# Batch 7's first product as seven half products over two column blocks, and batch 4's attention three slots earlier

## The chip, the cores and the metric

The kernel runs on one core of one Trainium2 chip. The metric is the device time of one execution in microseconds (us), the median over runs. Engines are named as in the profile: PE (matmul; PEld its weight loads), DVE (VectorE), ACT (ScalarE), POOL (GpSimd), SP (SyncE, which issues most DMAs).

## The reference

Eight batches of cosine-weighted linear attention, and then a mixer. Sequence 576, 8 heads of 64, model width 512, inner width 2048, rank 32.

```python
# attention, per batch and head (c, s: cos and sin of the position)
q_p = concat([relu(q) * c, relu(q) * s]);  k_p = concat([relu(k) * c, relu(k) * s])
kv = k_p.T @ v;  z = sum_s(k_p)
x = (q_p @ kv) / (q_p @ z + 1e-6)
# mixer, on x of shape [8, 576, 512]
h = x.transpose(0, 2, 1) @ U @ V          # U [576, 32], V [32, 576]
u = x + h.transpose(0, 2, 1)
out = u + relu(u @ w_ch1) @ w_ch2         # w_ch1 [512, 2048], w_ch2 [2048, 512]
```

The two products with w_ch1 ("first product") and w_ch2 ("second product") are nearly all of the matmul work.

## The kernel before

A batch's 576 rows are held as four chunks of 128 rows and a tail of 64; the tails of two batches make one block of 128 (a "pair", pr). All matmul operands are bf16, sums are fp32 in PSUM.

For each batch the attention makes q_p and k_p (`q_prep`, `k_prep`: DVE, ACT) from staged inputs `qst`, `kst`, `vst`; `v_prep` casts v to `v_ext` on POOL; SP issues DMA transposes of q_p (`qtr_dma`); `kv_unit` and `x_unit` are matmuls with their evacuation; `A_unit`, `u_mm` and `u_add` add the low-rank term and give u (`u_bf`, on DVE); `utr_dma` transposes u into `uT` (two DMAs, halves of the 512 columns); `u_tail` and `utr_dma(b, 4, 5)` do the same for the tails. `loads(b + 1)` issues the next batch's inputs on SP.

The first product of a batch (`g1_main`, L571) runs over 16 blocks j of 128 inner columns: four matmuls of 512 columns into one PSUM bank, then one ReLU on ACT (L580) into `hid`. `g1_tail` (L605) does a pair's tail: four groups of 16 matmuls of 128 columns, each into a bank of the "g" ring, each with one ReLU (L612).

The second product of batches 2 to 7 and of the last tails is already a scheme of Strassen and Winograd: `half_part` (L772) is one of seven half products of eight matmuls with 256 columns; `hid_sum` (L717) makes the sums of `hid` on DVE that it needs (S1, S2, and two in place); a join on DVE (L730) adds each half product to u.

The order is written by hand. `slots` is a list of thunks for PE's main work, one after the other; `todo` (filled by `put`) hangs other work behind a slot; `PLAN[b]` gives for each batch the slot w of its first `kv_unit` and the offsets of the rest, where a batch's q work begins at w - 20 and its u transposes follow w + 17. Batches 3 to 7 alternate: two blocks of `g1_main(b)`, then in turn one `half_part` of batch b - 1 and one block of `g1_main(b)`; after odd batches come four tail slots. Then the second product of batch 7 runs alone, and last that of the tails. Slot 88 is the first of batch 3's, 126 of batch 4's, 156, 190 and 220 of batches 5, 6 and 7.

Every engine works its queue in order. PSUM has eight banks: "g0", "g1" (ring of the first product), "g2" and "T" (attention), "o0", "o1" (second product), and the two of "X". A PSUM tile is one unit for waiting: who writes it next waits for all that read it.

Of the kernel before, what the change touches and what calls it, by code (L numbers as in the profile page):

```python
# [10 lines left out]
FP32 = mybir.dt.float32  # L11
BF16 = mybir.dt.bfloat16
AF = mybir.ActivationFunctionType
ALU = mybir.AluOpType
# [3 lines left out]
def kernel(  # L18
# [11 lines left out]
    nc = tc.nc  # L30

    B = 8
    H = 8
    S = 576
    D = 64
    E = D + 1
    P = 128
# [3 lines left out]
    NJ = DH // P  # L41
    NPAIR = B // 2
# [31 lines left out]
    ps = Banks()  # L74
# [1 line left out]
    ctx.enter_context(tc.manual_schedule())  # L76


    qst = const.tile([P, H, 5, D], FP32)
    kst = const.tile([P, H, 5, D], FP32)  # L80
    vst = const.tile([P, H, 5, D], FP32)

    def nines(src, b):
        return src[b].rearrange("h (m k) d -> m h (k d)", k=9)
# [25 lines left out]
    w1_bf = const.tile([P, 4, DH], BF16)  # L110
# [15 lines left out]
    def cast(eng, o, i):  # L126
        if eng is nc.scalar:
            nc.scalar.activation(out=o, in_=i, func=AF.Copy, bias=0.0, scale=1.0)
        else:
            eng.tensor_copy(out=o, in_=i)  # L130


    V_, A_, G_ = nc.vector, nc.scalar, nc.gpsimd
# [30 lines left out]
    def load_uv():  # L164
# [16 lines left out]
        out=iota[:, 0:4], pattern=[[2, 4]], base=0, channel_multiplier=9,  # L181
        allow_small_or_imprecise_dtypes=True,
    )
    for lo in (0, TS):
        nc.gpsimd.iota(
            out=iota[lo : lo + TS, 4:5], pattern=[[1, 1]], base=8, channel_multiplier=18,
# [3 lines left out]
        out=iota[:, 5:6], pattern=[[1, 1]], base=8, channel_multiplier=9,  # L190
# [85 lines left out]
    k_p, q_p, q_pT, kv_sb, x_bf = {}, {}, {}, {}, {}  # L276
    u_bf, u_tl, uT, uT_tl = {}, {}, {}, {}
# [279 lines left out]
    hid, hid_tl = {}, {}  # L557
# [35 lines left out]
                stop=False,  # L593
            )

    def g1_tail(pr, jq):
        if pr not in hid_tl:
            hid_tl[pr] = pool.tile(
                [P, NJ, P], BF16, tag="q_p" if pr == 3 else "hid_tl", bufs=1, name="hid_tl"
            )  # L600
        g_ps = ps.tile([P, 4, P], FP32, tag="g", bufs=3, name="gt_ps")
        for jj in range(4):
            j = jq * 4 + jj
            for d in range(4):
                nc.tensor.matmul(  # L605
                    out=g_ps[:, jj, :],
                    lhsT=w1_bf[:, d, j * P : j * P + P],
                    rhs=uT_tl[pr][:, d, :],
                    start=(d == 0),
                    stop=(d == 3),  # L610
                )
        nc.scalar.activation(  # L612
            out=hid_tl[pr][:, jq * 4 : jq * 4 + 4, :], in_=g_ps, func=AF.Relu,
            bias=0.0, scale=1.0,
        )
# [78 lines left out]
    def h_of(b, half, c):  # L694
        if b == B:
            return hid_tl[2 + c // 2][:, half * 8 : half * 8 + 8, :]
        return hid[b][:, half * 8 : half * 8 + 8, c * P : c * P + P]
# [45 lines left out]
    def half_part(b, n, k, form):  # L743


        c2 = n + 2
        i = ORDER[form][k]
        if k == 0:
            halves[b, n] = {
                "o": [  # L750
                    pool.tile([P, DM], FP32, tag="o_sb", bufs=8, name="o_sb") for _ in range(2)
                ]
            }
            if form == "alone":
# [12 lines left out]
        at = BANKS[form].get(i)  # L767
        if at is not None:
            w[to] = bank(at)
        acc = w[to][:, 0:256]  # L770
        for j in range(8):
            nc.tensor.matmul(  # L772
                out=acc, lhsT=lhs[:, j, :], rhs=rhs[:, j, :],
                start=(j == 0 and at is not None), stop=(j == 7),
                skip_group_check=at is None,
            )
        lo, hi = slice(0, 256), slice(256, 512)
        o, o2 = w["o"]
        u = [[u_of(b, c, g) for g in range(2)] for c in (n, c2)]

        def first(t, cs, c, g):
            add(V_, by_n(t[:, cs]), u[c][g], by_n(acc))

        def more(t, cs):
            add(V_, t[:, cs], t[:, cs], acc)

        if form == "alone":
            ss = w["s"]
            if i == 1:
                cast(A_, ss[:, lo], acc)  # L790
            elif i == 2:
                first(o, lo, 0, 0)
            elif i == 5:
                cast(A_, o2[:, hi], acc)
            elif i == 6:
                cast(A_, ss[:, hi], acc)
            elif i == 4:
                cast(A_, o2[:, lo], acc)
                add(G_, by_n(o2), by_n(o2), u_bf[b][:, :, c2, :])
            elif i == 3:  # L800
                first(o, hi, 0, 1)
                add(G_, o, o, ss)
            elif i == 7:
                o2v = o2.rearrange("p (g n) -> p g n", g=2)
                add(V_, o2v, o2v, acc.unsqueeze(1).to_broadcast([P, 2, 256]))
        elif i == 1:
            first(o, lo, 0, 0)
        elif i == 2:
            more(o, lo)
        elif i == 6:  # L810
            first(o, hi, 0, 1)
        elif i == 5:
            first(o2, hi, 1, 1)
        elif i == 3:
            more(o, hi)
        elif i == 4:
            first(o2, lo, 1, 0)
        else:
            if form == "last":
                more(o2, lo)  # L820
            more(o2, hi)
        if i == 2:
            hid_sum(b, n, 4)
        if k == 6:
# [37 lines left out]
    def spare(at):  # L862
# [8 lines left out]
    PLAN = {  # L871
        2: (46, -15, V_, V_, -10, (-5, -4, -4)),
        3: (64, -12, V_, A_, -7, (3, 3, 18)),
        4: (100, (-20, 1, V_, V_), (-13, 2, A_, V_), -12, (-9, -4, -4)),
        5: (127, (-24, 2, A_, A_), (-14, 2, A_, V_), -14, (-8, -4, -4)),
        6: (157, (-24, 2, A_, A_), (-14, 2, A_, V_), -14, (-8, -4, -4)),
        7: (191, (-24, 2, A_, A_), (-14, 2, A_, V_), -14, ()),
# [218 lines left out]
    for c in TL:  # L1096
        k_prep(0, c, FEATS[c])
        for h in range(H):
            nc.tensor.matmul(  # L1099
                out=z_ps[:, h : h + 1], lhsT=k_of(0, c, h), rhs=v_tl[:, 0, D:E],  # L1100
                start=(c == 0 and h == 0), stop=(c == 4 and h == H - 1),
            )
        if c < 4:
            nc.tensor.matmul(
                out=z_all[:, 1, :], lhsT=zero[:, 0:P], rhs=zero, start=True, stop=True
# [108 lines left out]
    def tail_out(pr):  # L1214
        slots.extend(lambda p=p: g2_part(pr, 4, p) for p in range(4))
# [10 lines left out]
    slots += [g1(2, j) for j in range(NJ)]  # L1226
    put(len(slots) - 1, lambda: ps.give("g", ("g0", "g1")))
    alone = len(slots)
    for b in range(3, B):
        at = len(slots)  # L1230
        sums(b - 1, 0, (at, at + 1, at + 3))
        sums(b - 1, 1, (at + 5, at + 7, at + 9) if b == 3 else (at + 13, at + 15, at + 19))
        slots += [g1(b, 0), g1(b, 1)]
        for n in range(2):
            for i7 in range(7):
                slots.append(lambda b=b, n=n, i7=i7: half_part(b - 1, n, i7, "with g"))
                if i7 > 4:
                    put(len(slots), lambda b=b, n=n, i7=i7: half_store(b - 1, n, i7 - 5))
                slots.append(g1(b, 2 + 7 * n + i7))
        if b % 2:  # L1240
            tail_slots(b // 2)
        if b == 3:
            tail_out(b // 2)
    at = len(slots)
    sums(B - 1, 0, range(at - 4, at - 1))
    sums(B - 1, 1, (at + 1, at + 3, at + 5))
    sums(B, 0, (at + 8, at + 10, at + 11))
    put(at - 1, lambda: ring.append("g2"))
    for n in range(2):
# [11 lines left out]
    at = len(slots)  # L1261
# [57 lines left out]
```

## Time and profile before

| | |
|---|---|
| median of 3 runs | 297.73 us (296.2 to 298.64) |
| profiled execution | 296.4 us, span 294.6 us |
| PE | 286.1 us busy (97% of the span) |
| DVE, ACT, POOL | 192.6, 154.7 and 51.1 us busy |
| clock that PE was granted | 1.0 throughout |
| matmuls of the first product, 128x512 | 0.379 us each, four in 0.86 us of the chain |
| matmuls of the second product, 128x256 | 0.273 us each, eight in 0.87 us of the chain |

A matmul's recorded duration holds its way through the array and overlaps with the next; what counts for PE is the step from one to the next. The chain of waits is followed back from the last instruction: at each step to what released it. "Idle before, releaser" tells how long an engine sat idle before an instruction and who ended it. A window's row gives busy time and counts of the engines in that stretch of the span.

### The profile page before, as it was taken

Reading aid. Unit: us, or ns where it says so; the run is one execution under the profiler, and the core shown is the slowest. Engines: PE = TensorE matmul, PEld = TensorE weight load, DVE = VectorE, ACT = ScalarE, POOL = GpSimd, SP = SyncE. Lnnn points to the kernel's source line nnn. Section 1 sums busy time; section 2 is a strip of 40 time slices with the busy share of each in tenths; the row PEclk is TensorE's granted clock in tenths of the full one; section 3 lists DMA queues with packets and bytes.
Section 4 is the critical chain, followed back from the end, with each engine's and each line's share of the span. In section 5 each row is a group of like instructions: output and inputs, shape, how many; then the busy total and the mean of one; then the engine's idle time right before and its main releaser. Section 6 shows DMA issues by size and latency. Waiting matters only on the chain.

```text
span 294.6 us, 6987 instructions
## 1 busy us (share of the span) xinstructions
PE 286.1 (97%) x2832; PEld 189.4 (64%) x2874; DVE 192.6 (65%) x459; ACT 154.7 (53%) x281; POOL 51.1 (17%) x89
## 2 busy tenths in 40 slices
PE   8999999999999999999989999999999999999995
PEld 6685464447645445676757666766877666668884
DVE  4978656684798887657546794678437755344563
ACT  2956842175880467577826865378743234334310
POOL 8800400012030002500500411031200100000340
PEclk9999999999999999999999999999999999999999
DMA  6999999799998999999989659952900141001013
GB/s 212 330 261 254 261 205 216 173 305 249 280 192 135 283 244 238 234 312 289 232 198 309 162 116 271 289 182 60 246 2 3 73 120 43 36 36 75 2 71 142
DMA packets 90707, 54.05 MB, mean 183 GB/s; under 512 B 58420, under 2 KB 87380, under 8 KB 90676
## 3 DMA queue, kind: packets, MB, share of 16 engines
q1 hardware_dynamic: 84116, 43.85, 62.4%
q0 software_dynamic: 6416, 9.63, 14.0%
q8 instruction: 22, 0.36, 0.5%
q10 hardware_dynamic: 144, 0.13, 0.1%
q14 instruction: 9, 0.07, 0.1%
HBM read 36.86 MB, written 9.44 MB: 157 GB/s over the span
## 4 chain that ended last, share of the span: by engine, by line
PE 94%; DVE 1%; DMA 1%; issue 1%; ACT 1%; SPq 0%; DVEq 0%
PE g_ps L571 36%; PE h_ps L772 27%; PE o_ps L643 10%; PE gt_ps L605 4%; PE w_ps L228 3%; PE kv_ps L342 3%; PE x_ps L417 3%; DMA uT<-u_bf 1%; PE a_ps L440 1%; PE t_ps L372 1%; PE va_ps L470 1%; PE t_ps L360 1%; PE g_ps L588 1%; DVE x_bf L427 0%; PE z_ps L1099 0%
## 5 line engine op out<-in xcount | busy, mean ns | idle before, releaser
L580 ACT ACTIVATE hid<-g_ps 128x512 bf16<-128x512 f32 x128 | 76.2, 597 | 100.9 <-PE g_ps L571 99.4
L571 PE MATMUL g_ps<-uT,w_bf 128*128 128x512 bf16 x474 | 121.1, 379 | 2.3 <-DMA uT<-u_bf 0.9
L571 PEld LDWEIGHTS <-w_bf 128*128 128x128 bf16 x504 | 47.5, 98 | 42.6 <-issue 1.1
L772 PEld LDWEIGHTS <-hid 128*128 128x128 bf16 x480 | 45.4, 98 | 11.8
L730 DVE TENSOR_TENSOR o_sb<-u_bf,h_ps 128x256 f32<-128x256 bf16 x44 | 18.4, 417 | 31.7 <-PE h_ps L772 31.5
L772 PE MATMUL h_ps<-w_bf,hid 128*128 128x256 bf16 x288 | 37.0, 273 | 0.1
L643 PE MATMUL o_ps<-w_bf,hid 128*128 128x512 bf16 x122 | 29.5, 379 | 0.4 <-issue 0.2
L130 POOL CAST v_ext<-vst 128x512 bf16<-128x512 f32 (+1 forms) x26 | 18.3, 729 | 57.3 <-DMA vst<-in_v_dram 46.8
L730 DVE TENSOR_TENSOR o_sb<-o_sb,h_ps 128x256 f32<-128x256 f32 (+1 forms) x36 | 15.5, 432 | 18.7 <-PE h_ps L772 18.5
L772 PE MATMUL h_ps<-w_s,S 128*128 128x256 bf16 x208 | 26.5, 273 | 0.0
L772 PE MATMUL h_ps<-w_s,hid 128*128 128x256 bf16 x192 | 24.9, 272 | 0.0
L830 POOL DMA_DIRECT2D out_dram<-o_sb x16 | 10.0, 625 | 84.4 <-DVE o_sb L730 83.0
L772 PEld LDWEIGHTS <-S 128*128 128x128 bf16 x208 | 19.9, 98 | 5.2
L478 DVE TENSOR_TENSOR u_bf<-x_bf,va_ps 128x512 bf16<-128x512 bf16 x27 | 17.8, 679 | 6.5 <-PE va_ps L470 4.2
L643 PEld LDWEIGHTS <-hid 128*128 128x128 bf16 x128 | 11.6, 98 | 12.5
L427 DVE TENSOR_TENSOR x_bf<-x_ps,rec 128x512 bf16<-128x512 f32 x22 | 15.2, 691 | 0.8
L605 PE MATMUL gt_ps<-uT_tl,w_bf 128*128 128x128 bf16 x256 | 15.6, 219 | 0.0
L605 PEld LDWEIGHTS <-w_bf 128*128 128x128 bf16 x256 | 14.7, 98 | 1.2
L301 ACT ACTIVATE k_p<-kst,cosw 128x512 bf16<-128x512 f32 x20 | 14.2, 713 | 0.4 <-DVE rec L408 0.4
L301 ACT ACTIVATE q_p<-qst,sinw 128x512 bf16<-128x512 f32 x18 | 12.6, 710 | 2.4 <-DMA qst<-in_q_dram 2.4
L303 DVE TENSOR_SCALAR k_p<-kst,sinw 128x512 bf16<-128x512 f32 x23 | 12.7, 554 | 0.0
L342 PEld LDWEIGHTS <-k_p 128*128 128x128 bf16 x240 | 10.5, 97 | 2.6
(170 smaller groups left out, 351.1 us busy)
## 6 DMA issues: line engine op xcount, KB each, us to landing
qst<-in_q_dram SPq DMA_DIRECT2D x14, 512.0 KB, 5.6
kst<-in_k_dram SPq DMA_DIRECT2D x14, 512.0 KB, 8.0
vst<-in_v_dram SPq DMA_DIRECT2D x12, 512.0 KB, 7.9
out_dram<-o_sb POOLq DMA_DIRECT2D x19, 256.0 KB, 3.4
w_bf<-in_moe_w_ch_dram POOLq DMA_DIRECT2D x8, 512.0 KB, 13.1
out_dram<-o_sb SPq DMA_DIRECT2D x16, 256.0 KB, 2.4
qst<-in_q_dram SPq DMA_DIRECT2D x2, 640.0 KB, 8.8
kst<-in_k_dram SPq DMA_DIRECT2D x2, 640.0 KB, 8.3
```

Source lines behind the costliest of these rows:

```text
L130: eng.tensor_copy(out=o, in_=i)
L301: nc.scalar.activation(out=o, in_=i, func=AF.Relu, bias=0.0, scale=w)
L303: eng.tensor_scalar(out=o, in0=i, scalar1=0.0, scalar2=w, op0=ALU.max, op1=ALU.mult)
L342: nc.tensor.matmul(out=acc[:, i, :], lhsT=k_of(b, c, h), rhs=v_tl[:, h, 0:n] if c == 4 and b < 2 else vx[:, c if c < 4 else 4 + b % 2, h, ...
L427: nc.vector.tensor_tensor(out=x_of(b, c, rows).rearrange("p (g i d) -> p g i d", g=2, d=D), in0=view[:, :, :, 0:D], in1=rec[rows].unsqueez ...
L478: nc.vector.tensor_tensor(out=u_bf[b][:, j, :, :], in0=x_bf[b][:, :, ns], in1=va[b][j].rearrange("p (c n) -> p c n", c=4), op=ALU.add,)
L571: nc.tensor.matmul(out=g_ps.rearrange("p (c t) -> p c t", c=4), lhsT=w1_bf[:, d, j * P : j * P + P], rhs=uT[b][:, d, :, :], start=(d == 0) ...
L580: nc.scalar.activation(out=hid[b][:, j, :], in_=g_ps, func=AF.Relu, bias=0.0, scale=1.0)
L605: nc.tensor.matmul(out=g_ps[:, jj, :], lhsT=w1_bf[:, d, j * P : j * P + P], rhs=uT_tl[pr][:, d, :], start=(d == 0), stop=(d == 3),)
L643: nc.tensor.matmul(out=o[:, cols], lhsT=lhs[:, j, c * P : c * P + P], rhs=w2_bf[:, j, cols], start=(j == 0), stop=(j == NJ - 1),)
L730: eng.tensor_tensor(out=o, in0=x, in1=y, op=ALU.add)
L772: nc.tensor.matmul(out=acc, lhsT=lhs[:, j, :], rhs=rhs[:, j, :], start=(j == 0 and at is not None), stop=(j == 7), skip_group_check=at is ...
```

## The change

Three things change.

1. Batch 7's first product. Blocks p and p + 8 are taken together with the two halves of the 512 rows and the two halves of the 512 inner indices d: seven half products (`g1_cross`) of two matmuls with 256 columns each, in place of eight matmuls with 512. They go into X and Y (the halves of one bank) and Z (half of another); even p use "g0" and "g1", odd p "g2" and "T". `g1_join` copies three of the partial results out (P1, U2, P5, on ACT), adds them to the others on DVE (C11, C22, C12), and makes the ReLUs (two on ACT, one clamp of 512 on DVE). Each group issues two or more half products of pair p and the rest of pair p - 1; between the groups stand batch 6's half parts, and between the last four groups the four tail blocks, which now lie two by two in the tile "X".
2. The sums that this needs: four of w_ch1 in two halves each (`w1_sum`, DVE, in slots 186 to 215) and four of uT (`uT_sum`, DVE, slots 218 to 221). They lie in the staging tiles of q, k and v, which batch 7 has read by then; the copies lie in the dead `q_pT`. For that the staging tiles come from the work pool.
3. In `PLAN`, batch 4's w goes from 100 to 97, with all that hangs on it.

```diff
-    qst = const.tile([P, H, 5, D], FP32)
-    kst = const.tile([P, H, 5, D], FP32)
-    vst = const.tile([P, H, 5, D], FP32)
+    qst, kst, vst = [
+        pool.tile([P, H, 5, D], FP32, tag=name, bufs=1, name=name)
+        for name in ("qst", "kst", "vst")
+    ]
...
+    W1 = [
+        w1_bf[:, 0:2, 0:1024], w1_bf[:, 2:4, 0:1024],
+        w1_bf[:, 0:2, 1024:2048], w1_bf[:, 2:4, 1024:2048],
+    ]
+    def w1_sum(i, half):
...
+        x, y, op = {
+            1: lambda: (W1[2], W1[3], ALU.add),
+            2: lambda: (w1_s[1], W1[0], ALU.subtract),
+            3: lambda: (W1[0], W1[2], ALU.subtract),
+            4: lambda: (W1[1], w1_s[2], ALU.subtract),
+        }[i]()
+        cs = slice(512 * half, 512 * half + 512)
+        diff(w1_s[i][:, :, cs], x[:, :, cs], y[:, :, cs], op)
...
+    CROSS = [("g0", "g1"), ("g2", "T")]
+    def g1_cross(b, p, i):
...
+            xy, z = [
+                psum.tile([P, 512], FP32, tag=tag, bufs=1, name="c_ps") for tag in CROSS[p % 2]
+            ]
+            cross[b, p] = {"X": xy[:, 0:256], "Y": xy[:, 256:512], "Z": z[:, 0:256]}
...
+        to, lhs, rhs, first = {
+            1: lambda: ("X", W1[0], uT_quarter(b, 0, 0), True),
+            2: lambda: ("Y", W1[1], uT_quarter(b, 1, 0), False),
+            3: lambda: ("Z", w1_s[4], uT_quarter(b, 1, 1), False),
+            4: lambda: ("X", W1[3], uT_s[b, 4], False),
+            5: lambda: ("Z", w1_s[1], uT_s[b, 1], True),
+            6: lambda: ("X", w1_s[2], uT_s[b, 2], False),
+            7: lambda: ("X", w1_s[3], uT_s[b, 3], False),
+        }[i]()
+        for d in range(2):
+            nc.tensor.matmul(
+                out=w[to].rearrange("p (c t) -> p c t", c=2), lhsT=lhs[:, d, cs],
+                rhs=rhs[:, d], start=(first and d == 0), stop=(d == 1),
+                skip_group_check=not first,
+            )
+    def g1_join(b, p, i):
+        w, lo, hi = cross[b, p], slice(0, 256), slice(256, 512)
+        top, low = hid[b][:, p, :], hid[b][:, p + 8, :]
...
+        if i == "C11":
+            diff(top[:, lo], w["P1"], w["Y"], ALU.add)
+        elif i == "C22":
+            diff(low[:, hi], w["P5"], w["X"], ALU.add)
+            relu(low[:, hi], low[:, hi])
+        elif i == "C12":
+            diff(top[:, hi], w["U2"], w["Z"], ALU.add)
+            relu(low[:, lo], w["X"])
+            V_.tensor_scalar(out=top, in0=top, scalar1=0.0, scalar2=None, op0=ALU.max)
+        else:
...
+            cast(A_, w[i], w["Z" if i == "P5" else "X"])
...
-        4: (100, (-20, 1, V_, V_), (-13, 2, A_, V_), -12, (-9, -4, -4)),
+        4: (97, (-20, 1, V_, V_), (-13, 2, A_, V_), -12, (-9, -4, -4)),
...
+    for i, half, sl in (
+        (1, 0, -4), (1, 1, -3), (3, 0, -3), (3, 1, -2), (2, 0, -1), (2, 1, 21), (4, 0, 22), (4, 1, 25),
+    ):
+        put(at - 30 + sl, lambda i=i, half=half: w1_sum(i, half))
+    for i in range(4):
+        put(at - 2 + i, lambda i=i: uT_sum(b7, i + 1))
...
+    def opened(p):      # products 1, 2; then P1, C11
+    def second(p):      # products 6, 5; then U2, P5
+    def third(p):       # product 7; then C22
+    def closed(p):      # products 3, 4; then C12
...
+    groups = [
+        group(p, *fs) for p in range(9) for fs in ((opened, third), (second, closed))
+    ]
...
+    def tail_cross(j):
+        if j % 2 == 0:
+            x_tail["t"] = ps.tile([P, 2, 512], FP32, tag="X", bufs=1, name="gt_ps")
...
+    for i, go in enumerate(groups):
+        slots.append(go)
+        if i < 14:
+            n, i7 = halfs[i]
+            slots.append(lambda n=n, i7=i7: half_part(b7 - 1, n, i7, "with g"))
...
+        else:
+            slots.append(lambda j=i - 14: tail_cross(j))
```

In the diff the four functions `opened` to `closed` are shortened to what they issue; `group(p, first, then)` runs `first(p)` and then `then(p - 1)`.

More of the change, by code (lines that the diff above doesn't have):

```diff
@@ L594, in g_half, with diff @@
             )
-    def g1_tail(pr, jq):
+    W1 = [
+        w1_bf[:, 0:2, 0:1024], w1_bf[:, 2:4, 0:1024],
+        w1_bf[:, 0:2, 1024:2048], w1_bf[:, 2:4, 1024:2048],
+    ]
+    w1_s, uT_s, cross = {}, {}, {}
+    def diff(o, x, y, op=ALU.subtract):
+        V_.tensor_tensor(out=o, in0=x, in1=y, op=op)
+    def w1_sum(i, half):
+        if i not in w1_s:
+            t = pool.tile(
+                [P, 2, 2, 1024], BF16, tag="qst" if i < 3 else "kst", bufs=1, name="w1_s"
+            )
+            for n in (0, 1):
+                w1_s[(i - 1) // 2 * 2 + 1 + n] = t[:, n]
+        x, y, op = {
[6 more added lines that the diff above has]
+        diff(w1_s[i][:, :, cs], x[:, :, cs], y[:, :, cs], op)
@@ new lines, in uT_quarter, with uT_sum @@
+    def uT_quarter(b, d, n):
+        return uT[b][:, 2 * d : 2 * d + 2, 2 * n : 2 * n + 2, :]
+    def uT_sum(b, i):
+        if i == 1:
+            t = pool.tile([P, 4, 2, 2, P], BF16, tag="vst", bufs=1, name="uT_s")
+            for n in range(4):
+                uT_s[b, n + 1] = t[:, n]
+        x, y = {
+            1: lambda: (uT_quarter(b, 0, 1), uT_quarter(b, 0, 0)),
+            2: lambda: (uT_quarter(b, 1, 1), uT_s[b, 1]),
+            3: lambda: (uT_quarter(b, 1, 1), uT_quarter(b, 0, 1)),
+            4: lambda: (uT_quarter(b, 1, 0), uT_s[b, 2]),
+        }[i]()
+        diff(uT_s[b, i], x, y)
@@ new lines @@
+    CROSS = [("g0", "g1"), ("g2", "T")]
+    def g1_cross(b, p, i):
+        if (b, p) not in cross:
+            if b not in hid:
+                hid[b] = pool.tile([P, NJ, 512], BF16, tag="hid", bufs=2, name="hid")
+            xy, z = [
+                psum.tile([P, 512], FP32, tag=tag, bufs=1, name="c_ps") for tag in CROSS[p % 2]
+            ]
+            cross[b, p] = {"X": xy[:, 0:256], "Y": xy[:, 256:512], "Z": z[:, 0:256]}
+        w = cross[b, p]
+        cs = slice(p * P, p * P + P)
+        to, lhs, rhs, first = {
[6 more added lines that the diff above has]
+            7: lambda: ("X", w1_s[3], uT_s[b, 3], False),
+        }[i]()
+        for d in range(2):
[3 more added lines that the diff above has]
+                skip_group_check=not first,
+            )
@@ new lines, in g1_join, with relu @@
+    def g1_join(b, p, i):
+        w, lo, hi = cross[b, p], slice(0, 256), slice(256, 512)
+        top, low = hid[b][:, p, :], hid[b][:, p + 8, :]
+        def relu(o, x):
+            nc.scalar.activation(out=o, in_=x, func=AF.Relu, bias=0.0, scale=1.0)
+        if i == "C11":
[8 more added lines that the diff above has]
+        else:
+            if (b, "kept") not in cross:
+                cross[b, "kept"] = pool.tile([P, 2, 3, 256], FP32, tag="q_pT", bufs=1, name="kept")
+            n = ("P1", "U2", "P5").index(i)
+            w[i] = cross[b, "kept"][:, p % 2, n]
+            cast(A_, w[i], w["Z" if i == "P5" else "X"])
@@ L597, in g1_tail @@
+    def g1_tail(pr, jq, g_ps=None):
         if pr not in hid_tl:
@@ L600, in g1_tail @@
             )
-        g_ps = ps.tile([P, 4, P], FP32, tag="g", bufs=3, name="gt_ps")
+        if g_ps is None:
+            g_ps = ps.tile([P, 4, P], FP32, tag="g", bufs=3, name="gt_ps")
         for jj in range(4):
@@ L1228 @@
     alone = len(slots)
-    for b in range(3, B):
+    for b in range(3, B - 1):
         at = len(slots)
@@ L1244, with group, go @@
     at = len(slots)
-    sums(B - 1, 0, range(at - 4, at - 1))
-    sums(B - 1, 1, (at + 1, at + 3, at + 5))
+    b7 = B - 1
+    for i, half, sl in (
[4 more added lines that the diff above has]
+        put(at - 2 + i, lambda i=i: uT_sum(b7, i + 1))
+    sums(b7 - 1, 0, (at, at + 1, at + 3))
+    sums(b7 - 1, 1, (at + 13, at + 15, at + 19))
+    def opened(p):
+        g1_cross(b7, p, 1)
+        g1_cross(b7, p, 2)
+        g1_join(b7, p, "P1")
+        g1_join(b7, p, "C11")
+    def second(p):
+        g1_cross(b7, p, 6)
+        g1_cross(b7, p, 5)
+        g1_join(b7, p, "U2")
+        g1_join(b7, p, "P5")
+    def third(p):
+        g1_cross(b7, p, 7)
+        g1_join(b7, p, "C22")
+    def closed(p):
+        g1_cross(b7, p, 3)
+        g1_cross(b7, p, 4)
+        g1_join(b7, p, "C12")
+    def group(p, first, then):
+        def go():
+            if p < 8:
+                first(p)
+            if p > 0:
+                then(p - 1)
+        return go
+    groups = [
+        group(p, *fs) for p in range(9) for fs in ((opened, third), (second, closed))
+    ]
+    halfs = [(n, i7) for n in range(2) for i7 in range(7)]
+    x_tail = {}
+    def tail_cross(j):
+        if j % 2 == 0:
+            x_tail["t"] = ps.tile([P, 2, 512], FP32, tag="X", bufs=1, name="gt_ps")
+        g1_tail(
+            NPAIR - 1, j, x_tail["t"][:, j % 2].rearrange("p (j t) -> p j t", j=4)
+        )
+    for i, go in enumerate(groups):
[3 more added lines that the diff above has]
+            slots.append(lambda n=n, i7=i7: half_part(b7 - 1, n, i7, "with g"))
+            if i7 > 4:
+                put(len(slots), lambda n=n, i7=i7: half_store(b7 - 1, n, i7 - 5))
+        else:
+            slots.append(lambda j=i - 14: tail_cross(j))
+    at = len(slots)
+    sums(b7, 0, (at - 1, at - 1, at))
+    sums(b7, 1, (at + 1, at + 3, at + 5))
     sums(B, 0, (at + 8, at + 10, at + 11))
```

## Prediction

> **What bounds the kernel now.** I read the page first (busy time, the chain that ended last), then what PE waited for, then tables by stage, then the two stages that the change touches in order of time.
>
> ```profile
> span 294.6 us, 6987 instructions
> PE 286.1 (97%) x2832; PEld 189.4 (64%) x2874; DVE 192.6 (65%) x459; ACT 154.7 (53%) x281; POOL 51.1 (17%) x89
> PE 94%; DVE 1%; DMA 1%; issue 1%; ACT 1%; SPq 0%; DVEq 0%
> ```
>
> PE is the bound: 94% of the chain, 97% busy. A matmul removed anywhere saves its issue time, but only if PE does not wait instead.
>
> ```profile
> PE g_ps L571 <- DMA uT<-u_bf: 0.9, 1, 0.9
> ```
>
> This is the only long PE wait after the first 2 us: 0.86 us at 149.8, where batch 4's first product waits for its second transposed half.
>
> The table by stage (us, then busy time and count of PE, PEld, DVE, ACT, POOL, clock, DMA share, GB/s): batch 7's first product beside batch 6's second, the tail blocks, and batch 7's second product alone.
>
> ```profile
> 242.10:269.20 27.10, 26.89 (x181) 17.80 (x184) 11.31 (x23) 9.55 (x16) 0.63 (x1) 1.00 0.13 50
> 269.20:272.80 3.60, 3.60 (x66) 3.59 (x64) 1.99 (x3) 2.39 (x4) 0.00 (x0) 1.00 0.20 75
> 272.80:291.20 18.40, 18.31 (x168) 16.17 (x166) 11.66 (x23) 3.67 (x9) 5.21 (x4) 1.00 0.17 65
> ```
>
> PE has no gap in the first, VectorE (DVE) and ScalarE (ACT) are idle for over half of it: that is the room the change wants to fill. The next view is ACT and DVE at its end:
>
> ```profile
> 269.24 0.60 ACT L580 ACTIVATE hid<-g_ps 128x512 bf16<-128x512 f32 x1 [1.14 <-PE g_ps L571]
> 270.13 0.60 ACT L612 ACTIVATE hid_tl<-gt_ps 128x512 bf16<-128x512 f32 x1 [0.30 <-PE gt_ps L605]
> 270.59 0.69 DVE L717 TENSOR_TENSOR S<-S,hid 128x1024 bf16<-128x1024 bf16 x1
> 271.20 0.69 DVE L717 TENSOR_TENSOR hid<-hid 128x1024 bf16<-128x1024 bf16 x1
> 273.68 0.38 ACT L128 ACTIVATE s_sb<-h_ps 128x256 f32<-128x256 f32 x1 [0.28 <-PE h_ps L772]
> ```
>
> Prices read here: ACT 0.60 for 128x512 and 0.38 for 128x256; ACT starts 0.20 after the issue of the last matmul ended (269.24 against 269.04, where the next group starts); a DVE sum of 1024 takes 0.69, but the next starts after 0.61, so 0.08 overlaps. The join of 128x256 (L730) is 0.42, so 0.34 in a queue. From ACT's end to DVE's start 0.03 is seen (243.79 to 243.82); towards PE I take 0.06.
>
> **The change part by part.**
>
> *Fewer columns.* Removed: 64 matmuls of 512 columns, 0.86 per four in the chain of waits (0.216 each), 13.8 us. Added: per pair of blocks seven half products of two matmuls with 256 columns, 112 in all, at 0.87 per eight (0.109, h_ps L772), 12.2 us. The 48 extra weight loads of 0.098 lie under 0.109 of matmul, as L772's do already. **-1.6 us**, if PE never waits.
>
> *More work per pair.* Instead of two ReLUs (1.2 us ACT) a pair gets three copies and two ReLUs on ACT (about 1.9) and three adds and one clamp on DVE. The clamp (512 bf16 in place) isn't in the trace: between 0.34 (half of a 1024 sum) and 0.47 (L303, 512 from f32); I take 0.35, nearer the bf16 row. DVE gets 8 x (3 x 0.42 + 0.35) + 4 x 0.42 = 14.6 us of recorded time on top of 11.31 in a stage of 25.5: full but for its overlaps. Every join now stands in that queue.
>
> *The pair's loop.* The order of instructions shows that product 6 waits for DVE: the sum C11, which needs the copy P1, which needs product 2. From product 2's issue: 0.20 + 0.38 + 0.03 + 0.42 + 0.06 = 1.09. PE's cover: product 7 of the pair before (0.22) and a half part (0.87) = 1.09. So about 0.02 per pair, and 0.1 in two pairs where a sum of `hid` (0.61) stands in front of C11. **+0.2**; bounds 0 (each step 0.05 shorter) and 0.27 a pair, 2.2 in all (each 0.05 longer).
>
> The Trainium skill, PSUM — Partial Sum Buffer, section "PSUM bank collisions raise a hardware error", says that two engines must not be in one bank at once and that waits go by bank, not by address. X and Y share a bank here, and the waits of the order are by bank, so the page speaks against this placing. Waits by address would drop C11 from the loop, and with it the two group starts below, some 1.4 us; no run shows it yet.
>
> *Start of the stage.* In group 0, ACT's 0.60 ReLU of batch 6's last block stands ahead of P1: product 6 comes 0.3 late. Then DVE has, from C11(0): C11, a sum of uT, S1, a join, a sum of uT, S2, a join, two sums of hid, C11(1): 0.34 + 0.34 + 0.61 + 0.34 + 0.34 + 0.61 + 0.34 + 0.61 + 0.61 + 0.42 = 4.6 us. PE meanwhile has 4 + 8 + 6 + 8 matmuls, 2.8 us, from 0.48 on. So it waits 4.6 + 0.06 - 3.3 = **1.3**, of it some 0.3 for S2 before the third half part and 1.0 at product 6 of pair 1. The uT sums (512 bf16) are unseen: 0.35 to 0.69, I take 0.42, near half the 1024 row; at 0.69, 0.5 more. Sum of both: **+1.6**, bounds 1.0 and 2.4.
>
> *Tail blocks.* Before, each took a ring bank of its own. Now two share one tile of two banks, and the order has the second, third and fourth wait for ACT, each for the ReLU of the block just before. After a block's last issue that is 0.20 + 0.60 + 0.06 = 0.86. PE's cover: two matmuls (0.22) before block 3, four (0.44) before block 4: waits of 0.64 and 0.42. Before block 2 there are eight (0.87), but ACT reaches ReLU 1 late, behind P1, C11, C22 and its clamp: 0.35. **+1.4**, bounds 1.1 and 1.7.
>
> *Sums of w_ch1.* Eight DVE sums of 1024, 0.61 each, in slots 186 to 215. The first five lie in and around batch 5's tail blocks, where DVE is busy 1.44 of 3.8 us; nothing waits. Without that cover S1 and S2 of batch 5 would be late by up to 3 us. Two stand before batch 7's last u_add: that ended at 237.84, and the tail product that needs its bank came at 238.46. 1.2 more, less 0.3 of idle in between, less 0.62: **+0.3**, bounds 0 and 0.6. uT's second transpose goes out 0.9 later on SP, still under a half part and product 1. The staging itself was dead.
>
> *Batch 4 three units sooner.* All its q and k work, three q transposes, kv, x, A, u and two u transposes move three slots (2.6 us) up, past batch 3's u_adds on DVE and, on SP, ahead of batch 5's second q transpose. The wait of 0.86 goes. But batch 4's v is not moved:
>
> ```profile
> 109.52 0.62 SPq L106 DMA_DIRECT2D vst<-in_v_dram  x1
> 110.24 0.61 SPq L93 DMA_DIRECT2D vst<-in_v_dram  x1
> 110.90 0.63 SPq L100 DMA_DIRECT2D vst<-in_v_dram  x1
> 117.11 3.94 POOL L130 CAST v_ext<-vst 128x512 bf16<-128x512 f32 x4 [2.82 <-DMA vst<-in_v_dram]
> ```
>
> POOL ends the casts at 121.05; kv came at 123.51 and will now be due at 120.9. And batch 3's u_adds now have two more pairs of q work (4 x 0.39) between them on DVE: its second u transpose leaves SP 1.6 later, batch 3's first product may wait 0 to 0.55 for it (I take 0.25), and v's loads, next on SP, land 0 to 1.6 later (DMA share there is over 1.0). Kv, and all of PE behind it, waits 0.1 to 1.7; I take 0.8. Net -0.86 + 0.25 + 0.8 = **+0.2**, bounds -0.8 and +1.4.
>
> Sum: -1.6 + 0.2 + 1.6 + 1.4 + 0.3 + 0.2 = **+2.1**. The profiled execution took 296.4 us (span 294.6 and 1.8 around it), so 298.5 on its own footing; the median of the runs shown is 297.73, 1.3 more, so **299.8**.
>
> **Rivals.**
> - *The waits are covered* (0.20): DVE and ACT run tighter than my queue sums, or PE's waits release sooner. For it: DVE idle for 16 us of the stage, and a loop that just closes. Against: the tail blocks' order, which no speed of DVE cures. Saved 1.6 + 0.86: 295.3 by the median, not slower.
> - *The pair's loop decides* (0.18): each of its steps 0.05 longer, which it is from 1.09 us on; product 6 then waits 0.27 in every pair, and the joins behind C11 follow. For: no slack at all. Against: prices without scatter in the rows. 2.0 more: 301.8, slower.
> - *Batch 4's v decides* (0.14): loads 1.6 late and casts as slow as now; kv waits 1.7, and x, A and u behind it give back what came sooner. For: DMA share over 1.0. Against: loads of 512 KB landed in 5.6 us at the median. 1.2 to 1.6 more: 301.2.
>
> **How the numbers follow.** The forecast, +0.9 to +3.0, has 0.48. One per cent, about what a measurement can tell here, is 3.0 us. Faster by that needs every wait covered and more: 0.04. Slower by that: the two slow rivals (0.32) and the upper end of the forecast (0.04): 0.36. The rest is 0.60. Range: down to a sum of lower bounds plus some scatter of the runs (296.2 to 298.64), 296.9; up past both slow rivals, 302.9.
>
> **What would show it.** Right: PE's waits after 240 name ACT hid_tl (three, together 1.4) and DVE hid (the largest, 1 us, in pair 1); the wait for uT at 149.8 gone; a new one of kv for POOL near 121; DVE near 25 us busy in the 25 to 29 us of the stage. Wrong: PE without gaps there (first rival); equal waits of 0.2 or more at product 6 in all eight pairs (second); over 1.5 at kv (third). The forecast falls if batch 7's stage, tail blocks included, takes no longer than the 30.7 us from 242.1 to 272.8.

## The result and the profile after

The changed kernel takes 298.4 us (median), the kernel before in the same comparison 296.79: a ratio of 1.0059, 95% interval 1.0034 to 1.0083, or 1.0 to 2.5 us more. Forecast were 2.1 us more, which lies inside this interval. The forecast of 299.8 us was 1.4 too high: 0.9 of that is the base (297.73 from three runs, 296.79 from twenty), 0.5 is the change. The profiled execution of the changed kernel, 300.97 us (span 299.2), was one of its slower ones, so it is read by stages and not by its total.

The page's first lines and its chain of waits:

```profile
span 299.2 us, 7180 instructions
PE 286.4 (96%) x2885; PEld 194.2 (65%) x2922; DVE 210.6 (70%) x503; ACT 157.6 (53%) x305; POOL 52.7 (18%) x89
PE 82%; DVE 7%; DMA 4%; issue 3%; ACT 1%; POOL 1%; SPq 1%; DVEq 0%; POOLq 0%; ACTq 0%
```

PE's share of the chain fell from 94% to 82%, DVE's rose from 1% to 7%. PE now waits for others, though for less than these shares suggest: it is still busy for 96% of the span. For whom, is in the list of PE's waits (us in total, times, longest):

```profile
PE g_ps L572 <- DMA uT<-u_bf: 2.2, 1, 2.2
...
PE gt_ps L706 <- ACT hid_tl L713: 0.9, 3, 0.5
PE c_ps L666 <- DVE hid L604: 0.8, 1, 0.8
PE kv_ps L343 <- POOL v_ext L131: 0.6, 1, 0.6
```

Three waits for `hid_tl` (tail blocks), one for `hid` (C11 of pair 1) and one of kv for the casts of v were named in the prediction. The first line was not: the wait for batch 4's `uT` should have gone, and it grew from 0.9 to 2.2. These times count from the modelled end of the last matmul; in steps of PE's issue a wait is 0.15 to 0.2 longer.

The table by stage, same columns as before. In the kernel before, batch 7's first product from 243.00, and its last tail blocks:

```profile
243.00:268.90 25.90, 25.69 (x173) 17.20 (x176) 10.89 (x22) 9.55 (x16) 0.63 (x1) 1.00 0.11 43
269.04:272.61 3.57, 3.57 (x66) 3.57 (x64) 1.99 (x3) 2.39 (x4) 0.00 (x0) 1.00 0.20 76
```

In the changed kernel, the groups, then from the first tail block on:

```profile
245.86:270.61 24.75, 23.75 (x212) 20.44 (x210) 19.96 (x51) 11.24 (x34) 0.63 (x1) 1.00 0.12 45
270.61:277.17 6.56, 5.61 (x80) 4.96 (x78) 3.07 (x8) 3.99 (x10) 0.00 (x0) 1.00 0.12 48
```

From the start of batch 7's first product (245.86; before 243.00, the block ahead at 242.13 and its 0.87) to the first matmul of the second product alone (277.17; before 272.61), the stage takes 31.31 us, before 29.61. That is 1.70 more; the prediction's terms for it, -1.6 + 0.2 + 1.6 + 1.4, make 1.6. DVE is busy for 23.0 us of it (19.96 + 3.07).

DVE's queue at the start of the stage, in order of time:

```profile
246.96 0.42 DVE L604 TENSOR_TENSOR hid<-kept,c_ps 128x256 bf16<-128x256 f32 x1 [0.55 <-ACT kept L129]
247.30 0.42 DVE L604 TENSOR_TENSOR uT_s<-uT 128x512 bf16<-128x512 bf16 x1
247.63 0.69 DVE L818 TENSOR_TENSOR S<-hid 128x1024 bf16<-128x1024 bf16 x1
...
248.91 0.68 DVE L818 TENSOR_TENSOR S<-S,hid 128x1024 bf16<-128x1024 bf16 x1
...
250.44 0.68 DVE L818 TENSOR_TENSOR hid<-hid 128x1024 bf16<-128x1024 bf16 x1
251.04 0.74 DVE L604 TENSOR_TENSOR hid<-kept,c_ps 128x256 bf16<-128x256 f32 x2
```

Each starts when the one before is done, without idle time, from C11 of pair 0 (246.96) to C11 of pair 1 (251.04 to 251.46): 4.5 us. PE's steps against it: product 6 of pair 0 issues at 247.44, 0.28 after the half part before it ended; the third half part waits 0.25 for S2; product 6 of pair 1 issues at 251.51, 0.99 after PE was done. Sum 1.52.

In the pairs behind, the wait for C11 stays, but is short. Pair 3:

```profile
257.24 1.04 PE L873 MATMUL h_ps<-w_s,hid 128*128 128x256 bf16 x8
258.17 0.60 PE L666 MATMUL c_ps<-uT_s,w_s 128*128 128x256 bf16 x4
```

The half part is issued by 258.11 (257.24 + 0.87), and product 6 follows 0.06 later. It is 0.06 to 0.08 in each of the pairs 2 to 6 and 0.04 in pair 7, together 0.38. The list of waits has none of these, since they end before the modelled end of the last matmul. From product 2's issue to product 6 this loop takes 1.15 (257.02 to 258.17), against a cover of 1.09 (product 7 of the pair before, 0.22, and the half part, 0.87).

The 0.28 of pair 0 is the same loop, and no matter of DVE's queue. No product 7 of an earlier pair stands in its way, so the cover is one half part, 0.87, and 1.15 - 0.87 = 0.28. The prediction laid it to ACT's ReLU of batch 6's last block. But P1 starts 0.26 after product 2's issue there (246.29 to 246.55), just as in pair 3 (257.02 to 257.28), where no ReLU stands ahead.

The tail blocks, in the chain of waits:

```profile
272.19 0.57 ACT hid_tl L713
...
272.80 1.07 PE gt_ps L706 x16
...
273.89 0.61 ACT hid_tl L713
...
274.54 1.07 PE gt_ps L706 x16
...
275.63 0.61 ACT hid_tl L713
```

Every block starts 0.04 after the ReLU of the block before. By PE's issue the three waits are 0.39, 0.63 and 0.41, together 1.43.

### The profile page after: what moved, and what is told of

Read it like the earlier page. It is cut to its first block, busy times and chain, and to the rows that moved or that the text cites. A ratio compares the mean times of both kernels' runs of the same rounds, so it can differ in the third digit from the quotient of the medians.

```text
span 299.2 us, 7180 instructions
## 1 busy us (share of the span) xinstructions
PE 286.4 (96%) x2885; PEld 194.2 (65%) x2922; DVE 210.6 (70%) x503; ACT 157.6 (53%) x305; POOL 52.7 (18%) x89
## 4 chain that ended last, share of the span: by engine, by line
PE 82%; DVE 7%; DMA 4%; issue 3%; ACT 1%; POOL 1%; SPq 1%; DVEq 0%; POOLq 0%; ACTq 0%
PE g_ps L572 27%; PE h_ps L873 25%; PE o_ps L744 8%; PE gt_ps L706 4%; PE c_ps L666 3%; PE kv_ps L343 3%; PE w_ps L229 3%; PE x_ps L418 3%; DMA vst<-in_v_dram 2%; DMA uT<-u_bf 2%; DVE q_p L304 2%; PE a_ps L441 1%; POOL v_ext L131 1%; DVE k_p L304 1%; ACT hid_tl L713 1%
## 5 line engine op out<-in xcount | busy, mean ns | idle before, releaser
L581 ACT ACTIVATE hid<-g_ps 128x512 bf16<-128x512 f32 x112 | 66.5, 597 | 88.8 <-PE g_ps L572 88.4
L572 PE MATMUL g_ps<-uT,w_bf 128*128 128x512 bf16 x415 | 105.3, 379 | 3.5 <-DMA uT<-u_bf 2.2
L572 PEld LDWEIGHTS <-w_bf 128*128 128x128 bf16 x440 | 41.9, 98 | 39.4 <-issue 2.8
L131 POOL CAST v_ext<-vst 128x512 bf16<-128x512 f32 (+1 forms) x26 | 20.0, 795 | 52.5 <-DMA vst<-in_v_dram 49.5
L706 PEld LDWEIGHTS <-w_bf 128*128 128x128 bf16 x256 | 15.0, 98 | 2.5 <-issue 1.5
L604 DVE TENSOR_TENSOR hid<-kept,c_ps 128x256 bf16<-128x256 f32 x24 | 9.4, 418 | 6.4 <-PE c_ps L666 3.8
L408 DVE TENSOR_SCALAR rec<-x_ps 128x8 f32<-128x8 f32 (+2 forms) x39 | 6.3, 162 | 10.6 <-PE x_ps L418 9.7
```

The source lines that it names most:

```text
L572: nc.tensor.matmul(out=g_ps.rearrange("p (c t) -> p c t", c=4), lhsT=w1_bf[:, d, j * P : j * P + P], rhs=uT[b][:, d, :, :], start=(d == 0) ...
L581: nc.scalar.activation(out=hid[b][:, j, :], in_=g_ps, func=AF.Relu, bias=0.0, scale=1.0)
L604: V_.tensor_tensor(out=o, in0=x, in1=y, op=op)
L706: nc.tensor.matmul(out=g_ps[:, jj, :], lhsT=w1_bf[:, d, j * P : j * P + P], rhs=uT_tl[pr][:, d, :], start=(d == 0), stop=(d == 3),)
```

## The experiments

"Stage" is the stretch of batch 7 just measured: 29.61 us before, 31.31 in the changed kernel. In `q5_later`, whose order is the changed kernel's from batch 6 on, it is 31.30, while medians move by some tenths; so small terms are read from the stage and not from the median.

**Which part costs: `b4_back` and `only_b4`.**

```diff
# b4_back, from the changed kernel
-        4: (97, (-20, 1, V_, V_), ...
+        4: (100, (-20, 1, V_, V_), ...
# only_b4, from the kernel before
-        4: (100, (-20, 1, V_, V_), ...
+        4: (97, (-20, 1, V_, V_), ...
```

> The changed kernel with batch 4's w back at 100; the half products, the sums and the tail blocks stay. Theory A, the sum of the prediction: batch 4's move is worth +0.2 us, the rest +1.9, so this is 1.9 us over the kernel before (ratio 1.006), and batch 7's stage with its tail blocks takes 31.3 us as in the changed kernel. Rival B: the profiled execution of the changed kernel is typical, where 1.9 us were lost around batch 4; then the half products are nearly even, and this is within 0.5 us of the kernel before (ratio below 1.002).

> The kernel before with one edit: batch 4's w at 97. Theory A: +0.2 us (ratio 1.0007): the wait of 0.86 for the second transposed half goes, and waits of about the same size come at batch 3's first product and at kv. Rival B: the wait doesn't go, it grows, since on SP a transpose of batch 5's q now stands between the two transposes of batch 4's u: +1.9 us (ratio 1.006), with PE's longest wait 1.5 to 2.5 us at batch 4's first product.

Measured: `b4_back` 298.58 us, ratio 1.0054 (1.0026 to 1.0083); `only_b4` 297.58 us, ratio 1.0025 (1.0005 to 1.0044). Rival B falls for the first: without batch 4's move the kernel is as slow as with it, and its stage takes 31.59 us. The 1.9 us lost around batch 4 in the changed kernel's profile are not typical. In `only_b4`, +0.7 us lies between A and B; its profile has one of theory A's two new waits, kv's. The other, at batch 3's first product, isn't there, and the wait for uT, which was to go, has only shrunk from 0.86:

```profile
PE kv_ps L342 <- POOL v_ext L130: 0.7, 1, 0.7
PE g_ps L571 <- DMA uT<-u_bf: 0.4, 1, 0.4
```

**The tail blocks: `tail_banks`.**

```diff
-        if j % 2 == 0:
-            x_tail["t"] = ps.tile([P, 2, 512], FP32, tag="X", ...)
-        g1_tail(NPAIR - 1, j, x_tail["t"][:, j % 2].rearrange(...))
+        if j in (1, 2):
+            t = psum.tile([P, 512], FP32, tag=("o0", "o1")[j - 1], ...)
+        else:
+            t = ps.tile([P, 2, 512], FP32, tag="X", ...)[:, 0]
+        g1_tail(NPAIR - 1, j, t.rearrange(...))
```

> The changed kernel with the four tail blocks in banks that don't wait for one another: the first and last in tile X, the second and third in o0 and o1, which batch 6's last half products have left. Theory A: the tail blocks' waits for the ReLU of the block before (hid_tl) are 1.4 us of PE's time; all go, and batch 7's stage falls from 31.3 to 29.9 us, the time by 1.4 (ratio 1.001 to the kernel before). Rival: ACT, which has two copies, two ReLUs and the tail's ReLU in each of these groups, is the bound there, so PE waits at the next half product for a copy instead, and less than 0.5 us is saved.

Measured: 296.62 us, ratio 0.9997 (0.9969 to 1.0025). All three waits for `hid_tl` are gone, the stage is 29.87 us, 1.44 less. ACT is not the bound there; the shared tile was.

**The transposes of batch 4's u: `q5_later`.**

```diff
-        5: (127, (-24, 2, A_, A_), (-14, 2, A_, V_), -14, ...
+        5: (127, (-24, 2, A_, A_), (-14, 2, A_, V_), -12, ...
```

> The changed kernel with batch 5's three q transposes two slots later, so that on SP none of the two long ones stands between the two transposes of batch 4's u. Theory: the second u transpose leaves SP within 1.5 us of the first (3.9 us in the changed kernel's trace, before 147.5), the wait of 2.2 us at batch 4's first product goes, and the time falls by 0.9 to 2.2 us (ratio 0.999 to 1.003). Rival: the transposes land late for another reason (queue of the DMA engines, u_adds on DVE), or batch 5's x units wait for their q instead: the time stays within 0.4 us of the changed kernel.

Measured: 297.9 us, ratio 1.0021 (1.0 to 1.0043); the wait for uT is gone, the second transpose leaves SP 2.8 us after the first (theory had 1.5), with only the short one of the tails between. But `tail_banks`, which has the changed kernel's order up to the tail blocks, has no such wait either. SP's transposes there in the changed kernel, and then in `tail_banks`:

```profile
142.27 1.23 SPq L514 DMA_TRANSPOSE uT<-u_bf  x1
143.61 3.82 SPq L387 DMA_TRANSPOSE q_pT<-q_p  x1
147.52 1.86 SPq L514 DMA_TRANSPOSE uT<-u_bf  x1
```

```profile
141.20 1.23 SPq L514 DMA_TRANSPOSE uT<-u_bf  x1
142.53 2.36 SPq L387 DMA_TRANSPOSE q_pT<-q_p  x1
144.98 1.41 SPq L514 DMA_TRANSPOSE uT<-u_bf  x1
```

The transpose of batch 5's q between them holds SP for 3.82 us in one execution and 2.36 in the other (1.83 in `start_order`, below), and the second u transpose goes out that much later. So the order theory names the right place, but what it costs varies from run to run: in the profiles with w at 97 (the two of `v_early` aside) the wait for uT was 2.2, 0.4, 0.5, 0.7 and three times under 0.2 (`q5_later` is one of these); with w at 100, 0.9, 0.3, 0.2 and 0.2. The gain of `q5_later` can't be told from this variation.

The hold on SP is only a part of it. The chain of waits has the way of the second u transpose from leaving SP to its landing, in the kernel before and in the changed one:

```profile
146.53 4.10 DMA uT<-u_bf
```

```profile
147.52 5.76 DMA uT<-u_bf
```

PE was done, and began to wait, at 149.82 (150.68 less 0.86) in the first and at 151.14 (153.32 less 2.18) in the second. So the transpose left 3.3 us ahead of that in the kernel before and 3.6 ahead in the changed one: no later for PE, but 1.7 us longer on its way. The other profiles say the same: from its leaving SP to PE's waiting matmul it is 4.15 to 4.51 us in the four with w at 100, and 5.18 to 6.31 in the five with w at 97 that show a wait there (`tail_banks`' is 0.09; the two of `v_early` aside). `y_bank` and `q5_later`, which don't wait, show only that it is under 4.9 and 5.9. With w at 97 a long transpose of batch 5's q leaves SP right behind it (149.47 in the changed kernel); with w at 100 both have left before. That the two then share the DMA engines would explain the longer way, but no run separates this.

**The start of the stage: `start_short` and `start_order`**, both from `tail_banks`.

```diff
# both: the third sum of batch 6's hid, behind C11 of pair 1
-    sums(b7 - 1, 0, (at, at + 1, at + 3))
+    sums(b7 - 1, 0, (at, at + 1, at + 4))
# start_short: uT's sums 3 and 4 on POOL (in uT_sum)
-        diff(uT_s[b, i], x, y)
+        (V_ if i < 3 else G_).tensor_tensor(out=uT_s[b, i], in0=x, in1=y, ...)
# start_order instead: uT's sums 2 to 4 in one go, in slot 219
-        put(at - 2 + i, lambda i=i: uT_sum(b7, i + 1))
+        put(at - 2 + (i > 0), lambda i=i: uT_sum(b7, i + 1))
```

> The kernel tail_banks with two edits to DVE's queue at the start of batch 7's stage: the sums 3 and 4 of uT go to POOL, and the third sum of batch 6's hid is put behind the sum C11 of pair 1. Theory, the prediction's queue of 4.6 us: it falls by 0.34 + 0.34 + 0.61 = 1.3, the wait of product 6 in pair 1 (0.8 us recorded, 1.0 in all) goes, and the time falls by 1.0 us against tail_banks, to 0.996 of the kernel before. Rival: POOL makes these sums slowly (its casts of the same size take 0.98 us) and product 7 of pair 0 waits for them, or DVE slows beside POOL: less than 0.4 us is saved.

> The kernel tail_banks with DVE's queue at the stage's start put in another order, all of it on DVE: uT's sums 2 to 4 one after the other ahead of C11 of pair 0, where DVE is idle for some 1 us, and the third sum of batch 6's hid behind C11 of pair 1. Theory, the prediction's queue of 4.6 us from C11 of pair 0 to C11 of pair 1: 0.34 + 0.34 + 0.61 less, so 3.3 us; the waits for S2 (0.3) and for C11 (1.0) go, batch 7's stage falls from tail_banks' 29.9 to 28.6 us, the time by 1.3 us to 0.996 of the kernel before. Rival: the waits are not DVE's queue but the loop of product 6 itself, and move on to pair 2: less than 0.4 us is saved.

Measured: `start_short` 297.53 us, ratio 1.0015 (0.9985 to 1.0046), stage 30.03: nothing gained, by its rival. POOL and DVE in its first 3 us:

```profile
245.79 1.17 POOL L639 TENSOR_TENSOR uT_s<-uT 128x512 bf16<-128x512 bf16 x1
246.19 0.42 DVE L604 TENSOR_TENSOR hid<-kept,c_ps 128x256 bf16<-128x256 f32 x1 [0.55 <-ACT kept L129]
246.53 2.10 DVE L818 TENSOR_TENSOR S<-hid 128x1024 bf16<-128x1024 bf16 x1
246.91 1.17 POOL L639 TENSOR_TENSOR uT_s<-uT,uT_s 128x512 bf16<-128x512 bf16 x1
```

DVE's sum of 1024, 0.68 or 0.69 us in the other rows, took 2.10: it ends 0.55 after POOL's second sum (246.53 + 2.10 against 246.91 + 1.17). What was taken off DVE's queue came back as one long instruction, and PE's recorded wait for S2 was 0.8 us (1.0 by its steps). The Trainium skill, SBUF — State Buffer, section "SBUF: two separate sides", says that DVE and GpSimd share one pair of ports as an exclusive lock, and that a DVE instruction with two inputs in SBUF has to wait for a GpSimd one that reads there and has started first. The trace agrees, and shows the other case too: the sum with two SBUF inputs was blocked, the join of 0.42 at 246.19, which has one input in PSUM, was not.

`start_order` has the same aim without POOL: 296.31 us, ratio 1.0002 (0.9974 to 1.003); its stage is 28.76 us, 1.11 under `tail_banks`, and the list of PE's waits has no DVE instruction for it. By PE's steps the 0.3 of pair 0 stays, and so do the short waits of the pair's loop; the wait for S2 is gone, and the 0.99 at product 6 of pair 1 is 0.08. So the queue was the cause, at 1.1 where 1.3 was expected. The median shows little of it; its profile has again 0.7 us of waiting for batch 4's uT, which `tail_banks`' has not. Theory's ratio of 0.996 lies outside the interval, so the gain on the whole time is not shown by this run.

**X and Y in one bank: `y_bank`**, from the changed kernel; its tail blocks lie by turns in a bank of the second product and in X.

```diff
-            cross[b, p] = {"X": xy[:, 0:256], "Y": xy[:, 256:512], "Z": z[:, 0:256]}
+            if (b, "Y") not in cross:
+                cross[b, "Y"] = ps.tile([P, 2, 512], FP32, tag="X", bufs=1, name="y_ps")
+            y = cross[b, "Y"][:, p % 2]
+            cross[b, p] = {"X": xy[:, 0:256], "Y": y[:, 0:256], "Z": z[:, 0:256]}
...
-            2: lambda: ("Y", W1[1], uT_quarter(b, 1, 0), False),
+            2: lambda: ("Y", W1[1], uT_quarter(b, 1, 0), True),
```

> The changed kernel with Y, the place of product 2, in a bank of tile X instead of the half of X's bank, and the tail blocks by turns in a bank of the second product and in X. Product 6 then has no wait for the sum C11, whatever the granularity of waits. Theory: the start falls from 1.6 to 0.3 us (the wait for S2 alone stays), the tail blocks from 1.4 to 0, so 2.7 us less than the changed kernel and 1.3 less than tail_banks: 0.995 of the kernel before. Rival: DVE's queue is what is late, and the wait comes back at products 3 and 4, behind the copies and sums that end later: about even with tail_banks, 0.999.

Measured: 296.64 us, ratio 0.9993 (0.9969 to 1.0016); stage 29.44, 0.43 under `tail_banks`. PE's waits in it:

```profile
PE c_ps L669 <- DVE hid L604: 0.5, 1, 0.5
...
PE h_ps L876 <- DVE S L821: 0.4, 1, 0.4
```

Product 6 waits no more; the wait stands at product 4 of pair 0, behind C22, which ends just as late (0.66 by PE's steps). The short waits of the pair's loop are gone. The rival holds in the main: DVE's queue was late, and the shared bank only said where PE met it.

**All together: `combined` and `combined_y`.** The first is `start_order`, the second `y_bank` with `start_order`'s edits to DVE's queue, and both have

```diff
-        (1, 0, -4), ... (2, 0, -1), (2, 1, 21), (4, 0, 22), (4, 1, 25),
+        (1, 0, -4), ... (2, 0, -1), (2, 1, 25), (4, 0, 26), (4, 1, 27),
-        4: (97, (-20, 1, V_, V_), ...
+        4: (100, (-20, 1, V_, V_), ...
```

> start_order with batch 4's w back at 100 and the last three sums of w_ch1 behind batch 7's last u_add. Theory: start_order's gain, and 0.2 us for the tail product of batch 7's u, which the trace of the changed kernel showed 0.23 late; batch 4's move is worth some tenths either way: 0.5 to 1.5 us under the kernel before, ratio 0.995 to 0.998. Rival: nothing of that is left, as with start_short: 1.000.

> The same edits on y_bank in place of tail_banks: Y in a bank of tile X. Theory: with DVE's queue short, product 6 hangs on C11 no more in either kernel, and the placing of Y is worth only the 0.3 us of group 0 and the pair's loop (0.2): 0.3 to 0.5 us under combined. Rival, that the shared bank of X and Y costs 1.4 us by itself: more than 1 us under combined.

Measured: `combined` 296.4 us, ratio 0.9991 (0.9965 to 1.0017), stage 29.03, with one wait of product 6 for C11 in pair 3 (0.17 recorded, 0.34 by steps). The sums of w_ch1 cost nothing there: from batch 7's first u product to the block of slot 219 it is 10.20 us, as before, and 10.43 in the changed kernel. `combined_y` 295.08 us, ratio 0.9955 (0.9928 to 0.9983), stage 28.19: faster than the kernel before by 0.5 to 2.1 us, and than the changed one. Its stage by the table of stages:

```profile
243.12:271.31 28.19, 28.19 (x290) 25.49 (x289) 22.59 (x59) 15.40 (x44) 0.63 (x1) 1.00 0.13 50
```

By its steps PE has one gap of over 0.03 in it, 0.17 at 249.18, where product 1 of pair 2 waits for its bank. The own bank for Y is worth 0.84 us of the stage here (1.3 by the medians, whose intervals overlap), more than theory's 0.3 to 0.5 and, in the stage, less than the rival's 1. The steps say where from: `combined` loses 0.30 in pair 0 and 0.73 in the pair's loop (0.34 of it in pair 3), `combined_y` only its 0.17. C11 is late by some 0.06 in every pair (1.15 against 1.09), and the separate bank takes it out of the loop.

**The loads of v: `v_early` and `v_early_again`** (the same code), from `only_b4`.

```diff
-        3: (64, -12, V_, A_, -7, (3, 3, 18)),
+        3: (64, -12, V_, A_, -7, (3, 3, 14)),
```

> The kernel before with batch 4's w at 97 and its loads of v four slots sooner, which puts them on SP ahead of batch 3's u transposes. Theory: kv's wait for POOL's casts (0.7 us in only_b4) was the loads that left SP at 112 us, behind those transposes; they now leave before 105 and the wait goes: 0.7 us less than only_b4, ratio 1.000. Rival: POOL's casts are the limit, or the loads then share the DMA engines with batch 3's u transposes and these land later, with a wait at batch 3's first product: ratio 1.0025 as in only_b4.

> v_early once more, the same code. In its first profile PE waited at 70 and 90 us already, before the edit can act, and the DMA queue's share of 30 to 95 us was 0.96, against 0.82 in only_b4 with the same bytes. If that was the chip's state at the time, this comes out at 0.999 to 1.003 of the kernel before. If the early loads of v are to blame, it stays at 1.011, with the share again over 0.9.

Measured: 300.1 us, ratio 1.0112 (1.0076 to 1.0149), and 300.13, ratio 1.0125 (1.0073 to 1.0177). Kv's wait near 121 us went in both, and the kernel is some 2.5 us slower than `only_b4` (300.1 against 297.58). The second profile has the rival's wait, at batch 3's first product:

```profile
PE g_ps L571 <- DMA uT<-u_bf: 4.2, 3, 2.4
```

Two of the three are at 115.5 and 117.0 us (2.43 and 0.90): batch 3's u transposes, which now leave SP behind 1.2 MB of v. The third, 0.89, and the longest of the first profile, 1.45, are at batch 4's first product. The first profile has only 0.25 at batch 3's, and waits of 0.3 to 0.4 at 70 and 90 us, before the edit can act. Why these came, and why the DMA queue was busier then (0.96, in the second 0.88, against 0.82), stays open; the second run speaks against the chip's state alone.

## Why the prediction was right, and where not

| term | predicted | measured |
|---|---|---|
| fewer columns | -1.6 | -1.6: `combined_y`'s stage, 28.19 less its one gap of 0.17, against 29.61 |
| pair's loop | +0.2 | +0.4: 0.06 to 0.08 in each of five pairs, 0.04 in the last; 0.34 in one pair of `b4_back` and of `combined` |
| start of the stage | +1.6 | 0.28 + 0.25 + 0.99 = 1.5; 1.1 of it gone by order alone |
| tail blocks | +1.4 | 0.39 + 0.63 + 0.41 = 1.43; 1.44 gone in banks of their own |
| sums of w_ch1 | +0.3 | 0.23; gone in `combined` |
| batch 4 | +0.2 | +0.7 (0.15 to 1.3) alone; beside the rest +0.1, give or take 1.1 (1.0059 against 1.0054) |

The sum of the first four was 1.6 and is 1.70. The pair's loop is the smallest of them and the worst in proportion: ACT started P1 0.26 after product 2's issue ended (257.02 to 257.28) and not 0.20, and so each pair lost 0.06 where 0.02 was taken. The 0.3 for pair 0 was right in size by luck: it was put down to ACT's ReLU, and is the missing cover. The place of each wait came out too: product 6 in pairs 0 and 1, S2 ahead of the third half part, the ReLU of the tail block before. For the tail blocks even each single wait did (0.35, 0.64 and 0.42). What carried this were queue sums on the steps that engines really take (0.34 for a join, 0.61 for a sum), not on recorded durations. The two prices that no row showed were right or a little high: uT's sums 0.42, as taken; the clamp 0.30 instead of 0.35. DVE's busy time in the stage is 23.0 and not near 25: recorded durations overlap (their sum is 25.8), and were added. One price was read from the wrong row: the 5.6 us to landing, named against the third rival, is that of q's loads; the same page has 7.9 for v's. No term of the sum used it.

The sums of w_ch1: the time from batch 7's first u product to the block of slot 219 grew from 10.20 us (231.93 to 242.13) to 10.43 (234.57 to 245.00), and is 10.42 in `b4_back` and `tail_banks`.

The step that failed is "The wait of 0.86 goes". It was priced from one execution, as a fixed sum that a move of 2.6 us must clear. In its place the wait was 2.18 in the changed kernel's profile and 0.44 in `only_b4`'s. Of the two waits put against it, the 0.25 at batch 3's first product came in none of the profiles with w at 97, `v_early`'s aside. The one of kv held in the changed kernel's: the loads of v left SP 1.6 us later, the casts ran to 122.6, and kv waited.

```profile
111.09 0.62 SPq L107 DMA_DIRECT2D vst<-in_v_dram  x1
...
118.67 3.94 POOL L131 CAST v_ext<-vst 128x512 bf16<-128x512 f32 x4 [4.19 <-DMA vst<-in_v_dram]
```

The prediction saw that all of batch 4's attention moves up SP's queue, but took from it only that the u transposes pass batch 5's second long q transpose. The first one still stands between the two, and where it held SP for 3.82 us, the second u transpose left at 147.52 (144.98 in `tail_banks`; before 146.53). And it had no term for a longer way to the landing: from leaving SP to PE's waiting matmul it was 4.15 us in the kernel before and 5.80 in the changed one; why, stays open. So the term is the balance of two waits that vary from one execution to the next, that for uT from under 0.1 to 2.2 and kv's between none (four of seven profiles) and 0.75, and +0.2 was right in size by luck as much as by its working; its upper bound of 1.4 took in the +0.7 of `only_b4`.

Of the rivals, "the waits are covered" falls with the waits and the stages shown above; "the pair's loop decides" has its wait in every pair, but at 0.06 to 0.08 and not at 0.27; "batch 4's v decides" falls with kv's 0.6, of which 1.7 was asked. The remark that waits by address would save some 1.4 us was too high: Y in a bank of its own, which does at least as much, saved 0.43 while DVE's queue was late, and 0.84 when it wasn't.

## What to carry to other kernels

Seven products for eight pay only what PE saves when nothing waits, here 1.6 us; the adds and copies must then fit as queues, in order, where the stage begins and where it ends, and not as busy shares. Both of these edges cost about as much as the whole gain, and both were cured, all but 0.17 us, by order and by PSUM places alone, without one instruction less. A wait for a DMA that one execution shows is a sample: price a move past it by the queue's order, and give it the spread that other executions show.

## What the hardware showed that was not expected

- A POOL sum beside a DVE sum with both inputs in SBUF stretched the DVE one from 0.69 to 2.10 us; a DVE join with one input in PSUM kept its 0.42.
- The second transpose of batch 4's u took 4.1 us from leaving SP to landing in the kernel before and 5.76 in the changed one; a later q transpose went out right behind it only in the second. No run shows that this is the cause.
- The same q transpose held SP's queue for 1.83, 2.36 and 3.82 us in three executions of the same order, and what stood behind it was late by as much.
- Putting 1.2 MB of loads ahead of two transposes in SP's queue cost 2.5 us, where it was to save 0.7.
